# Eleven plain attention tiles instead of thirteen, and a new order of all operations

## The chip, the cores and the metric

The kernel runs on one core of a Trainium2 chip. The metric is the device time of one execution in microseconds. Three executions of the kernel before took 955.89, 956.62 and 960.74 us; the median is 956.62 us.

## What is computed

Inputs are q, k and v of 8 batches, 8 heads, 576 positions and 64 features in float32, and two weight matrices of 512x2048 and 2048x512 in float64. The reference, cut to what matters:

```python
scores = q @ k.T / 8                       # per batch and head
scores = where(0 <= row - col < 64, scores, -1e9)
attn = exp(scores - max); attn = attn / (sum(attn) + 1e-9)
x = (attn @ v), heads side by side         # 8 x 576 x 512
u = x + real(fft(fft(x, axis=1), axis=2))
un = (u - mean(u)) / sqrt(var(u) + 1e-6)   # over the 512 features
out = u + relu(un @ w_ch1) @ w_ch2
```

## The kernel before

The 4608 rows (8 batches of 576) are cut into 36 tiles of 128 rows; nine tiles make a pair of batches. Four kinds of work follow each other for each batch, and all of them share the engines:

- **attn_tile(T)**, 36 times: loads k, q and v of one tile, computes scores against the tile's own keys and the 64 before, the softmax, and the product with v. It also sums the four quarters of the features (`radix4`), and turns the result so that features lie along partitions (`flip_y` or `y_turn`).
- **fft(b)**, 8 times: both Fourier transforms of one batch as matrix products, written to a DRAM tensor `md`.
- **norm_tile(T)**, 36 times: gathers the rows of `md`, adds them to x, normalises, splits the result into two 16-bit parts and turns it by a DMA transpose (`u_turn`, L1271) into `uhl`, the input of the feed-forward part.
- **ffn(c)** and, for the last chunks, **ffn7(c)**: 18 chunks of two tiles each. In chunks 1 to 10 the first product is `bank1` (L1459, 16 groups of 12 matmuls) and the second is `second` (L1439, 16 groups of 6 for each half). Chunk 0 uses float32 weights. `weight_piece` makes float32 of the float64 weights on VectorE, and `weight_split` (L1414) makes two 16-bit parts.

An attention tile has two forms, chosen by `whole = T < PRO` in `attn_tile`:

- A **plain** tile (T below PRO) works in float32. TensorE transposes k and q against an identity (L491, four matmuls each), writes the mask into the score banks (L620, two) and adds the scores (L625, 32 float32 matmuls). VectorE takes the minimum (L644), ScalarE the exponentials (L657). TensorE transposes the probabilities (L674, eight), multiplies by v (L727, 32 float32 matmuls) and transposes the result (L840, four).
- A **split** tile writes every operand as a high and a low 16-bit part: the high part is a cast (L426 or L430, on ScalarE or VectorE), the low part a subtraction (L506, L517, L688 on GpSimd or VectorE; L561 on VectorE for v). The transposes of k, q, both halves of the probabilities and the result are five DMA transposes issued by SyncE. TensorE does the scores (L611, 32 float16 matmuls) and the product with v (L727, 48 float16 matmuls). VectorE does mask and minimum in one pass (L646, eight). Two copies per tile (`q_swap`) put q's low part beside its high part.

At T == PRO a few one-off operations turn the last plain tile's keys and values into two parts (`k_tail`, L546 to L549, and `v_tail`, L581 and L582), and `to_parts` negates the mask (L410).

The order of the instructions is made when the program is built. Each operation is given to `Plan.op` with an engine (or two to choose between, with a margin), a duration in us, the buffers it reads and writes, and a priority on a scale of us: `PITCH * T` for a tile, offsets for its steps, 60 and on for the weight splits, 1e6 and more for the feed-forward products, so that these come last. `Plan.order` is a list scheduler: it takes the operation that can start first by its model, and among these the one with the lowest priority. What it gives is a fixed order for every engine; on the chip each engine runs its list in that order and waits where an operand is late. In this schedule the feed-forward products fill TensorE wherever nothing of the other kinds is ready; where the model sees a gap before them, filler matmuls (`warm`, L1949) are put in.

Three tables change priorities without touching the work: `NUDGE` adds to the priority of the k-th operation of a kind, `LEAD` adds to all operations of a kind for one tile, piece or chunk, and `BIAS` adds to the margin by which the second engine is chosen. The key lookup that the change relies on is

```python
lead = LEAD.get({"split": "whole", "odd": "even", "first": "even"}.get(self.kind, self.kind), ())
prio += NUDGE.get(self.kind, {}).get(self.k, 0.0) + (lead[self.at] if self.at < len(lead) else 0.0)
```

and the choice between two engines is

```python
sooner = max(free[e2], s2) + d2 + o.margin < max(free[e1], s1) + d1
```

Of the kernel before, what the change touches and what calls it, by code (L numbers as in the profile page):

```python
# [41 lines left out]
LAZY_E, LAZY_Y = 0.3, 0.8  # L42
WARM = 0.8, 0.4
EARLY, LATER = 80, -20
PRO = 13
PITCH, FFT_AT, NORM_AT, FFT1 = 8.5, 13, 6, 0
SLACK = 0.0
SLACK_V = 0.3
WARY = 0
LAZY_N = 0.2  # L50
LAZY_S = 0.2
LAZY_Q = 0.1
LAZY_X = 1.0
# [12 lines left out]
ACT_NORM = 4  # L66
C_AT = ("fh", "fh", "pt", "pt")
NUDGE = {
    "": {0: 3.6, 1: 16.6, 2: -0.4, 3: 15.9, 4: 69.4, 5: 25.3, 6: -12, 8: 0.2, 10: 3.8, 11: -27.5},
}  # L70
LEAD = {
}
BIAS = {
}
VS = 64.0
YS = 32.0
# [78 lines left out]
class Plan:  # L155
# [21 lines left out]
    def op(self, eng, dur, prio, fn, reads=(), writes=(), lat=0.0, alt=(), holds=(), port=True, lock=True):  # L177

        o = Op()
        lead = LEAD.get({"split": "whole", "odd": "even", "first": "even"}.get(self.kind, self.kind), ())
        prio += NUDGE.get(self.kind, {}).get(self.k, 0.0) + (lead[self.at] if self.at < len(lead) else 0.0)
        o.group = (self.kind, self.at, self.k)
        bias = BIAS.get(self.kind, {}).get(self.k, 0.0)
        self.k += 1
        o.durs = {e: d + self.FIXED[e] for e, d in ([(eng, dur), alt[:2]] if alt else [(eng, dur)])}
        o.port, o.slack, o.wary, o.lock = port, self.slack, self.wary, lock
        o.margin = (alt[2] if len(alt) > 2 else self.MARGIN) + bias
        o.eng, o.dur, o.lat, o.fn, o.prio, o.margin = eng, dur, lat, fn, round(prio, 3), round(o.margin, 3)  # L190
        o.idx, o.outs, o.allocs = len(self.ops), [], []
        deps = set()
        for b in reads:
            deps.update(b.writers)
        for b in writes:
            deps.update(b.writers)
            deps.update(b.readers)
            if b.ring and not b.writers and b not in o.allocs:
                o.allocs.append(b)
        for b in holds:  # L200
            if b.ring and not b.held:
                o.allocs.append(b)
            b.held = True
        o.bufs = list({id(b): b for b in (*reads, *writes, *holds)}.values())
        for b in o.bufs:
            b.left += 1
        for b in reads:
            b.readers.append(o)
        for b in writes:

            b.writers.append(o)
        deps.discard(o)
        o.deps = deps
        self.ops.append(o)
        return o
# [116 lines left out]
def attn_fft_ffn_kernel(ctx: ExitStack, tc: tile.TileContext, q, k, v, w1, w2, gidx, dft_d, dft_s, mask, out):  # L332
# [72 lines left out]
    def to_parts():  # L405
# [5 lines left out]

        op("POOL", 0.4, PITCH * PRO - 25, negate, writes=[Bmskb], lock=False)

# [21 lines left out]
    def attn_tile(T, base):  # L435
        pb, n = divmod(T, NT)
        b0, i = 2 * pb, T % 2
        own, old = T % 3, (T + 1 if T == PRO else T - 1) % 3

        whole = T < PRO  # L440
        lazy = plan.MARGIN if whole else LAZY
# [27 lines left out]

        before = (T + 1 if T == PRO else T - 1) % 3  # L470
        kst_ = (kst32 if whole else kst16)[:, T % 3 * kw : (T % 3 + 1) * kw].rearrange("p (h s) -> p h s", s=P)
# [63 lines left out]
        was = plan.k  # L535
        if T == PRO and n > 0:

# [35 lines left out]
        was = plan.k  # L573
        if T == PRO:
            last = (T - 1) % 3
# [162 lines left out]

        op("DVE", 0.62, base + 6.25, normed, [bpa, brc], [bx], alt=("ACT", 2.6, LAZY_N), port=False)
        plan.k += 1  # L740
# [1240 lines left out]
```

## Time and profile before

| | us |
|---|---|
| executions, three | 955.89, 956.62, 960.74 |
| the profiled execution's own time | 960.97 |
| its span, first to last instruction | 959.2 |
| TensorE busy | 940.1 (98%) |
| VectorE busy | 806.8 (84%) |
| ScalarE busy | 588.5 (61%) |
| GpSimd busy | 297.0 (31%) |
| mean granted TensorE clock | 0.996 |

PE is TensorE, PEld its weight loads, DVE VectorE, ACT ScalarE, POOL GpSimd, SP SyncE, which issues nearly all DMAs. "L727" is line 727 of the kernel, and tile names stand as out<-in. Busy times of matmuls are modelled with their pipeline's tail, so two groups in a row overlap a little; in the chain of waits the steps are counted from start to start and do not overlap.

### The profile page before, as it was taken

To read this page: it belongs to the slowest core of one execution; us is meant where nothing else is said; L and a number is where in the kernel's file an instruction comes from. 1 tells how busy PE (TensorE), PEld (TensorE's weight loads), DVE (VectorE), ACT (ScalarE), POOL (GpSimd) and SP (SyncE) were. 2 spreads that over 40 slices of the span, in tenths; PEclk is the share of its full clock that TensorE was granted. 3 is DMA by queue.
4 is the path that set the end of the run, shared out by engine and by line. 5 is a ranking of instruction groups with operands and counts; after the bars stand their busy time and mean duration, and the time that the engine had idled before them with its cause. 6 is when DMAs were issued, how large, how long until landed. Compare 5 with 4: busy or idle time off the path is not lost.

```text
span 959.2 us, 25735 instructions
## 1 busy us (share of the span) xinstructions
PE 940.1 (98%) x10209; PEld 729.7 (76%) x10209; DVE 806.8 (84%) x1894; ACT 588.5 (61%) x1540; POOL 297.0 (31%) x335
## 2 busy tenths in 40 slices
PE   8999999999999999999899999999999999999997
PEld 6777767767776767677676676676688999999996
DVE  4989898998977988977986997989977688888685
ACT  6866768887767586866576773343454555645352
POOL 1111020343534342523422352332110254534040
PEclk9999999999999999999999999999999999999999
DMA  8979941599899699989969563312123213222000
GB/s 192 298 175 272 284 110 45 140 168 204 166 217 201 148 204 190 213 179 204 166 164 204 116 150 91 100 28 75 25 65 80 60 62 74 59 81 43 21 23 24
DMA packets 302697, 127.60 MB, mean 133 GB/s; under 512 B 281064, under 2 KB 281704, under 8 KB 302576
## 3 DMA queue, kind: packets, MB, share of 16 engines
q1 hardware_dynamic: 299712, 116.91, 55.0%
q0 software_dynamic: 2720, 8.92, 3.5%
q8 instruction: 80, 1.31, 0.6%
q14 instruction: 41, 0.34, 0.1%
q10 hardware_dynamic: 144, 0.13, 0.0%
HBM read 62.85 MB, written 22.04 MB: 89 GB/s over the span
## 4 chain that ended last, share of the span: by engine, by line
PE 76%; DVE 10%; DMA 6%; ACT 3%; issue 3%; POOL 2%; POOLq 0%; SPq 0%; DVEq 0%; ACTq 0%
PE ph L1459 19%; PE po L1439 18%; PE q L1815 11%; PE py L1707 5%; PE ph L1680 4%; PE px L1707 4%; PE pa L727 2%; PE pz L1047 2%; PE psc L611 2%; PE pg L995 2%; DMA out<-xu 2%; PE pp L674 1%; DMA xu<-xd 1%; PE psc L625 1%; ACT pr L657 1%
## 5 line engine op out<-in xcount | busy, mean ns | idle before, releaser
L1439 PE MATMUL po<-w1s,hh 128*128 128x512 f16 (+1 forms) x1024 | 264.5, 393 | 0.0
L1459 PE MATMUL ph<-uhl,w0s 128*128 128x256 f16 (+1 forms) x2040 | 263.2, 279 | 0.0
L1459 PEld LDWEIGHTS <-w0s 128*128 128x128 f16 x1920 | 186.5, 98 | 50.5 <-issue 1.1
L1439 PEld LDWEIGHTS <-hh 128*128 128x128 f16 x960 | 91.4, 98 | 81.3 <-issue 1.2
L1198 POOL DMA_INDIRECT mt<-md,gix x34 | 41.9, 1233 | 127.9 <-DVE xu L1211 58.4
L1471 ACT ACTIVATE hh<-ph 128x512 f16<-128x512 f32 x80 | 47.2, 590 | 49.7 <-PE po L1439 24.7
L1474 DVE SCALAR_TENSOR_TENSOR hh<-ph,hh 128x512 f16<-128x512 f32 x80 | 54.6, 683 | 21.1 <-ACT hh L1471 20.8
L657 ACT ACTIVATE pr<-pr,nm 128x128 f32<-128x128 f32 x184 | 71.3, 391 | 1.4 <-DVE nm L646 1.2
L1815 PEld LDWEIGHTS <-qbd 128*128 128x128 f16 x672 | 64.7, 98 | 9.1 <-DVE qbd L1779 1.1
L1815 PEld LDWEIGHTS <-kst 128*128 128x128 f16 x504 | 49.2, 98 | 5.7
L1779 DVE TENSOR_TENSOR flex<-flex 128x256 f32<-128x256 f32 x92 | 39.9, 434 | 9.5 <-ACT flex L1750 3.7
L430 POOL COPY yp<-y 128x1024 uint16<-128x1024 uint16 x23 | 25.5, 1109 | 70.7 <-DVE y L762 58.1
L1707 PEld LDWEIGHTS <-wa 128*128 128x128 f16 x750 | 45.9, 98 | 0.2
L1707 PEld LDWEIGHTS <-w0s 128*128 128x128 f16 x720 | 44.9, 98 | 0.2
L646 DVE CUSTOM_DVE_ANT_0 pr<-psc,mskb 128x128 f32<-128x128 f32 x184 | 42.0, 283 | 2.3 <-PE psc L611 2.2
L1680 PE MATMUL ph<-uhl,w0s 128*128 128x256 f16 x384 | 43.7, 273 | 0.0
L1224 POOL TENSOR_TENSOR rs<-mv,mhalf 128x1 f32<-128x1 f32 x36 | 26.1, 726 | 55.1 <-DVE mv L1220 52.5
L1815 PE MATMUL q<-w1s,qbd 128*128 128x256 f16 x336 | 41.4, 273 | 1.4 <-DVE qbd L1779 0.9
L1680 PEld LDWEIGHTS <-w0s 128*128 128x128 f16 x384 | 37.6, 98 | 5.4
L1792 ACT CAST qbd<-flex 128x1024 f16<-128x1024 f32 x28 | 29.2, 1044 | 19.6 <-DVE flex L1779 11.6
L1707 PE MATMUL py<-uhl,wa 128*128 128x128 f16 x570 | 41.0, 219 | 0.0
L426 ACT COPY v<-v 64x1024 uint16<-64x1024 uint16 x25 | 26.1, 1044 | 23.8 <-PE pa L727 20.9
(278 smaller groups left out, 2147.9 us busy)
## 6 DMA issues: line engine op xcount, KB each, us to landing
wd<-in_moe_w_ch SPq DMA_DIRECT2D x26, 512.0 KB
out<-xu SPq DMA_DIRECT2D x34, 256.0 KB
kn<-in_k SPq DMA_DIRECT2D x32, 256.0 KB
qn<-in_q SPq DMA_DIRECT2D x32, 256.0 KB
xd<-xa SPq DMA_DIRECT2D x30, 256.0 KB
xu<-xd SPq DMA_DIRECT2D x30, 256.0 KB
flex<-in_v SPq DMA_DIRECT2D x20, 256.0 KB
md<-mp SPq DMA_DIRECT2D x24, 192.0 KB
```

The lines of the kernel that those rows point to most:

```text
L646: nc.vector.tensor_tensor_reduce(out=t["pr", jj][:, hp], in0=t["ps", jj][:, hp], in1=mskb[:, m : m + P], scale=-0.125, scalar=3.0e38, op0= ...
L657: nc.scalar.activation(pr, src, AF.Exp, bias=t["nm", jj][:, hp : hp + 1], scale=-1.0, accum_out=t["rc"][:, hp, jj])
L1198: nc.gpsimd.indirect_dma_start(out=mts[T], out_offset=None, in_=mds[pb][0 : HR if n < 4 else 2 * HR], in_offset=bass.IndirectOffsetOnAxis( ...
L1439: nc.tensor.matmul(t["po"][i], l_, r_, start=(f == 0 and x == 0), stop=(f == NKF - 1 and x == len(mm) - 1))
L1459: nc.tensor.matmul(ph, l_, r_, start=(x == 0), stop=(x == len(mm) - 1))
L1471: nc.scalar.activation(t["hh", pr][:, 0], ph, AF.Relu)
L1474: nc.vector.scalar_tensor_tensor(out=hh[:, 1], in0=ph, scalar=0.0, in1=hh[:, 0], op0=ALU.max, op1=ALU.subtract)
L1680: nc.tensor.matmul(ph, l_, r_, start=(x == 0), stop=(x == len(mm) - 1))
L1707: nc.tensor.matmul(to[:, x], l_(a, k_), r_(b_, k_), start=(y == 0), stop=(y == 5))
L1779: return lambda eng=nc.vector: eng.tensor_tensor(out=o, in0=a, in1=b, op=al)
L1792: op("ACT", 0.95, -9, lambda h4=h4, oa=oa: nc.scalar.copy(oa[:, 0], h4), Bh4, [Boa])
L1815: nc.tensor.matmul(t["q"][q_][:, y], l_[:, a, i, m], r_(b_, m), start=(s_ + y + m + x == 0), stop=(s_ == 3 and m == 1 and x == 2 and (y == ...
```

## The change

`PRO` goes from 13 to 11: tiles 11 and 12 are made as split tiles. `LAZY_N`, the margin by which the scaling of the attention output (`normed`) goes to ScalarE rather than VectorE, goes from 0.2 to -0.8. The three tables get entries for nearly all kinds of operations.

```diff
-PRO = 13
+PRO = 11
...
-LAZY_N = 0.2
+LAZY_N = -0.8
...
 NUDGE = {
-    "": {0: 3.6, 1: 16.6, 2: -0.4, 3: 15.9, 4: 69.4, 5: 25.3, 6: -12, 8: 0.2, 10: 3.8, 11: -27.5},
+    "": {0: 14.4, 1: 16.6, 2: -0.4, 3: 15.9, 4: 69.4, 5: 25.3, 6: -12, 8: 0.2, 10: 3.8, 11: -27.5},
+    "even": {14: -0.3},
+    "ffn7": {16: -0.6, 232: 0.3, 1276: 3.2, 2005: 0.6, 2006: 0.7, 2047: 12.4, 2100: -0.7, 2120: 1.3, 2141: -0.3, 2145: -0.1, 2146: 0.5, 2167: 0.2},
+    "first": {21: 0.8, 32: -0.1, 62: 1.2},
+    "odd": {34: -2.9},
+    "piece": {0: 10.6},
+    "split": {3: -0.1, 25: -0.2},
 }
 LEAD = {
...
+    "norm": (
+        0, 0, 0, 0, 0, 0, 0, 0, 0, 0.4, 0, 0, 0, 0, 2.6, 2.6,
+        3.9, 3.9, 3.9, 4, 3.9, 4.1, 3.9, 3.9, 3.9, 3.9, 3.9, 3.9, 3.9, 3.9, 3.9, 3.9,
+        3.9, 3.9, 3.9, 3.9,
+    ),
+    "part": (
+        0.3, 0.3, 0.3, 0.3, 0.3, 0.3, 0.3, 0.3, 0.3, 0.3, 0.3, 0.3, 0.3, 0.3, 0.3, 0.3,
+        0.3, 0.3, 0.3, 0.3, -1.7, 0.3, 0.3, 0.3, 0.3, 0.3, 0.3, 0.3, 0.3, 0.3, 0.3, 0.3,
+    ),
+    "piece": (
+        0, 0, 0, 0, 0, 0, 0, 0, 0, 0, 0, 0, 0, 0, 0, 0,
+        0, 0, 0, 0, 0, 0, 0, 0, 0, 0.1, 0, 0.8, 0.8, 0.8, -9.9, -9.9,
+    ),
...
+    "whole": (
+        0, 0, 0, 0, -1.5, -1.5, -1.5, -1.5, -2.9, -2.9, -2.9, -2.9, -2.9, -2.9, -2.9, -2.9,
+        -2.9, -2.9, -2.9, -2.9, -4.6, -2.9, -2.9, -2.9, -2.9, -2.9, -2.9, -2.9, -2.9, -2.9, -2.9, -2.9,
+        -2.9, -2.9, -3.1, -3.1,
+    ),
 }
 BIAS = {
+    "ffn7": {21: -0.4},
+    "first": {13: -0.8},
 }
```

The tables left out here hold zeros only.

## Rows read from the trace of the kernel before

**Rows 1.** Busy time of engines by stage: window, length, each engine, PEclk, DMA share, GB/s.
```profile
0.00:87.00 87.00, 81.71 (x956) 62.52 (x957) 68.51 (x144) 61.00 (x215) 16.01 (x25) 1.00 0.86 229
87.00:130.00 43.00, 43.00 (x295) 30.76 (x295) 39.00 (x80) 28.05 (x92) 4.48 (x4) 1.00 0.81 236
130.00:190.00 60.00, 59.45 (x499) 42.93 (x499) 55.21 (x111) 47.79 (x115) 12.45 (x11) 1.00 0.39 99
190.00:214.00 24.00, 23.70 (x233) 16.12 (x231) 21.98 (x70) 20.80 (x62) 10.73 (x15) 1.00 0.88 177
214.00:460.00 246.00, 244.87 (x2849) 174.81 (x2847) 207.26 (x588) 173.58 (x467) 99.19 (x110) 1.00 0.98 191
460.00:520.00 60.00, 54.76 (x610) 39.76 (x609) 51.04 (x151) 41.09 (x113) 18.76 (x20) 0.94 0.84 178
520.00:955.00 435.00, 432.57 (x4779) 362.84 (x4776) 362.97 (x754) 216.18 (x480) 134.83 (x150) 1.00 0.28 67
```
**Rows 2.** What TensorE waited for: total us, times, longest.
```profile
PE pg L995 <- DVE hs L955: 3.9, 4, 2.9
PE pa L727 <- DMA pt<-flex: 2.0, 1, 2.0
```
**Rows 3.** Chain of waits, plain tiles on TensorE, 123 to 178: start, us, what.
```profile
123.94 0.87 PE pp L674 x8
...
131.88 0.44 PE pk L491 x4
...
139.86 0.43 PE psc L620 x2
140.29 1.03 PE psc L625 x32
...
176.33 1.08 PE pa L727 x32
```
**Rows 4.** The same chain, split tiles and chunk 1's last products, 204 to 220.
```profile
204.90 0.57 PE psc L611 x16
...
215.37 1.29 PE po L1439 x6
...
217.97 0.88 PE pa L727 x48
218.85 0.90 PE psc L611 x32
```
**Rows 5.** Instructions by line: count, busy us, mean ns, idle before them.
```profile
L646 DVE CUSTOM_DVE_ANT_0 pr<-psc,mskb 128x128 f32<-128x128 f32 x184 | 42.0, 283 | 2.3 <-PE psc L611 2.2
...
L644 DVE TENSOR_REDUCE nm<-psc 128x4 f32<-128x512 f32 x26 | 16.8, 683 | 12.2 <-PE psc L625 12.2
...
L561 DVE SCALAR_TENSOR_TENSOR v<-flex,v 128x512 f16<-128x512 f32 x23 | 18.8, 819 | 2.2 <-ACT v L559 2.2
...
L688 DVE TENSOR_TENSOR flex<-pr,flex 128x512 f16<-128x512 f32 x26 | 20.6, 801 | 1.6 <-ACT flex L426 1.3
...
L688 POOL TENSOR_TENSOR flex<-pr,flex 128x512 f16<-128x512 f32 x20 | 25.7, 1286 | 25.7 <-ACT flex L426 17.7 <-DVE flex L430 6.3 <-DVE sw L1532 1.6
```
**Rows 6.** Timeline, VectorE and GpSimd, 165 to 168: start, us, what.
```profile
165.01 0.75 DVE L1414 SCALAR_TENSOR_TENSOR w1s<-w1s,s 128x512 f16<-128x512 f32 x1
...
166.85 1.70 DVE L1414 SCALAR_TENSOR_TENSOR w0s<-w0s,s 128x512 f16<-128x512 f32 x1
166.84 1.15 POOL L517 TENSOR_TENSOR flex<-qn,flex 128x512 f16<-128x512 f32 x1 [27.39 <-DVE flex L430]
```
**Rows 7.** Timeline around chunk 2's start: SyncE's issue of its last transpose, TensorE's first use.
```profile
207.72 1.24 SPq L1271 DMA_TRANSPOSE uhl<-up  x1
...
213.90 1.47 PE L1459 MATMUL ph<-uhl,w0s 128*128 128x256 f16 x12
```
**Rows 8.** Chain of waits, DMA transposes at 290 and 505, issue to landing.
```profile
290.75 4.95 DMA uhl<-up
...
505.58 6.03 DMA pt<-flex
```

More of the change, by code (lines that the diff above doesn't have):

```diff
@@ L68 @@
 NUDGE = {
-    "": {0: 3.6, 1: 16.6, 2: -0.4, 3: 15.9, 4: 69.4, 5: 25.3, 6: -12, 8: 0.2, 10: 3.8, 11: -27.5},
+    "": {0: 14.4, 1: 16.6, 2: -0.4, 3: 15.9, 4: 69.4, 5: 25.3, 6: -12, 8: 0.2, 10: 3.8, 11: -27.5},
[5 more added lines that the diff above has]
+    "split": {3: -0.1, 25: -0.2},
 }
 LEAD = {
+    "": (
+        0,
+    ),
+    "even": (
+        0, 0, 0, 0, 0, 0, 0, 0,
+    ),
+    "ffn7": (
+        0, 0, 0, 0, 0, 0, 0, 0, 0, 0, 0, 0, 0, 0, 0, 0,
+        0, 0,
+    ),
[7 more added lines that the diff above has]
+        0.3, 0.3, 0.3, 0.3, -1.7, 0.3, 0.3, 0.3, 0.3, 0.3, 0.3, 0.3, 0.3, 0.3, 0.3, 0.3,
+    ),
+    "piece": (
+        0, 0, 0, 0, 0, 0, 0, 0, 0, 0, 0, 0, 0, 0, 0, 0,
+        0, 0, 0, 0, 0, 0, 0, 0, 0, 0.1, 0, 0.8, 0.8, 0.8, -9.9, -9.9,
+    ),
+    "pre1": (
+        0, 0, 0, 0,
+    ),
+    "prep": (
+        0, 0, 0, 0,
+    ),
+    "scale": (
+        0, 0,
+    ),
+    "tail": (
+        0, 0, 0, 0, 0, 0, 0, 0, 0, 0, 0, 0,
+    ),
+    "whole": (
+        0, 0, 0, 0, -1.5, -1.5, -1.5, -1.5, -2.9, -2.9, -2.9, -2.9, -2.9, -2.9, -2.9, -2.9,
+        -2.9, -2.9, -2.9, -2.9, -4.6, -2.9, -2.9, -2.9, -2.9, -2.9, -2.9, -2.9, -2.9, -2.9, -2.9, -2.9,
+        -2.9, -2.9, -3.1, -3.1,
+    ),
 }
 BIAS = {
+    "ffn7": {21: -0.4},
+    "first": {13: -0.8},
 }
```

## The prediction

> **What bounds the kernel now.** I read the busy times by stage first, then what TensorE waited for, then the chain of waits. In the stages the reader is to see that TensorE is the full engine from 87 us on: 43.00 of 43, 59.45 of 60, 23.70 of 24, 244.87 of 246, and 432.57 of 435 from 520 to 955 [rows 1]. One stage is different: from 460 to 520 it is busy for 54.76 of 60 at a granted clock of 0.94. The waits name the two stalls in it: 3.9 us for an FFT operand (2.9 of them at once), 2.0 us for a transposed probability tile [rows 2]. Before 87 us, 81.71 of 87 are busy, but this includes filler matmuls; there the chain through attention tiles, the first FFT and the weights sets the pace. So, from 87 us on, a matmul that is taken out shortens the run by its length, provided that the list behind it can move up. The second engine to watch is VectorE: 39.00 of 43, 55.21 of 60 and 21.98 of 24, which leaves 4.00 + 4.79 + 2.02 = 10.8 us of idle time between 87 and 214 [rows 1]. The two tiles that change form lie there.
>
> **Part 1: TensorE loses work.** A plain tile costs, from start to start in the chain: k turned 0.44, q and the result, four matmuls of the same shape each, 0.44 each; mask 0.43; scores 1.03; probabilities turned 0.87; product with v 1.08 [rows 3]. The sum is 4.73 us. A split tile costs 0.90 for its scores in one piece, or 2 x 0.57 in two, and 0.88 for the product with v [rows 4]: 1.78 to 2.02, middle 1.90. One tile saves 2.71 to 2.95, two save 5.4 to 5.9; I take 2 x 2.83 = 5.7 us. All of these matmuls lie after 105 and before 214, where TensorE is full, so they are on the path.
>
> **Part 2: VectorE, ScalarE, GpSimd and DMA gain work.** On VectorE, mask and minimum take 8 x 42.0/184 = 1.83 us per tile instead of 2 x 16.8/26 = 1.29, so 0.54 more; the low part of v adds 18.8/23 = 0.82; the low parts of k, q and the two halves of the probabilities are four subtractions of one shape, 20.6/26 = 0.79 each on VectorE or 25.7/20 = 1.29 each on GpSimd [rows 5]. On GpSimd they are not free for VectorE: the subtraction at 166.84 held GpSimd for 1.15 us, and the weight split that VectorE started beside it took 1.70 instead of 0.75 [rows 6]. So a tile adds between 0.54 + 0.82 + 4 x 0.79 = 4.5 and 0.54 + 0.82 + 4 x 1.29 = 6.5 us of VectorE's time, two tiles 9.0 to 13.0. Some copies out of PSUM that VectorE did for plain tiles fall away, and the new `LAZY_N` sends scalings to ScalarE, which has 12.21 us idle in 130 to 190 against VectorE's 4.79 [rows 1]. I take the lower end, 9.0, which the 10.8 us of idle time hold; then this costs nothing. If it does not fit, the price is in the third rival.
>
> The Trainium skill has a rule that speaks against this part, in "SBUF — State Buffer", section "Who interferes with whom": VectorE and GpSimd share one pair of ports, held for a whole instruction, and the loser waits instead of sharing. The 1.70 us agree. By the rule all eight low parts would cost VectorE 1.29 each wherever they run, and part 2 would come to 13.0.
>
> The DMA side gets ten more transposes, and no load falls away. One takes 1.24 us of SyncE's time to issue [rows 7] and 4.95 us from issue to landing in a crowded stretch [rows 8], so ten take between 12 and 50 us of the queue. From 130 to 190 the DMA engines are busy 0.39 of the time, which leaves 37 us [rows 1]. I take 30, about the middle, which that gap hides. Without the cover (from 190 on the share is 0.88, then 0.98) a transpose lands as late as the one at 505, 6.03 us after issue, and that one was the stall of 2.0 us [rows 8, 2].
>
> **Part 3: what is late next.** TensorE would reach the products of chunk 2 5.7 us earlier, at 213.90 - 5.7 = 208.2, but their last operand leaves SyncE only at 207.72 [rows 7] and lands, at 4.95 us [rows 8], at 212.7. Uncovered, that is a wait of 4.5 us, and the change would keep 1.2 us. The cover is what stands behind chunk 2's start and needs nothing of it: two groups of chunk 1's second product, 1.29 each, and the attention products of 0.88 and 0.90 [rows 4], together 4.4 us, which can go first. Moving the FFT of batch 1 and the gathers of tiles 4 and 5 up would serve as well. I cost this at nothing, between 0 and 4.5.
>
> **Part 4: the new order.** The tables add no instruction. They redraw the whole list, so the small stalls fall elsewhere. What they can win after 87 us is what TensorE does not use now: 5.24 us idle from 460 to 520, with up to 0.06 x 60 = 3.6 us lost to the clock, together 8.8; 2.43 after 520; 1.98 between 87 and 460 [rows 1]. What they can lose I bound by as much again, 8.8. The `norm` entries of 3.9 make the gathers of tiles 16 and on later against the rest, and those of `whole` make attention earlier; both move work inside a stretch that TensorE fills with feed-forward products anyway. In the first 87 us at most the 5.29 idle us and some fillers could go. I take nothing for part 4, the middle between its ends, since the rows show no stall that the model must have seen.
>
> **The sum.** The profiled execution took 960.97 us, of which 959.2 are the span. 960.97 - 5.7 = 955.3. The median of the three executions is 4.35 us lower than this one, 956.62, and the saved matmuls are the same in any of them: 956.6 - 5.7 = 950.9 us.
>
> **The rivals.**
>
> The first: the order also removes the stalls of 460 to 520. For it speaks that both hang on one late operand each; against it that the list is fixed from a model which did not see them. Time: 950.9 - 8.8 = 942.1.
>
> The second: the gate in part 3 is not covered. TensorE arrives early at chunk 2 and waits for the transposed rows of tile 5. For it speaks that the operand's landing at 212.7 is only 1.2 us ahead of its use now, and that VectorE, which makes it, is at 92% from 130 to 190. Against it, the 4.4 us of products that can go first. Time: 956.6 - 1.2 = 955.4.
>
> The third, on the other side: VectorE cannot hold the extra work between 87 and 214. At 13.0 us against 10.8 of idle time it no longer fits, and one tile's 6.5 us standing ahead of the FFT of batch 1 puts the landing off to 212.7 + 6.5 = 219.2. TensorE, with the 4.4 us of part 3, is done at 208.2 + 4.4 = 212.6 and waits 6.6 us. The clock's loss comes on top: in 460 to 520 it was up to 3.6 for 5.24 idle us [rows 1], so here up to 4.5. Against the saving of 5.7 this is +5.4 us: 962.0. It decides where VectorE's added work passes its idle time by more than the 2 to 3 us that the copies and scalings give back. For it speaks [rows 6]; against it that tile 12 has a lower claim in the list than the FFT of batch 1.
>
> That the edit would leave the two tiles plain is excluded by `whole = T < PRO`.
>
> **How the numbers follow.** 0.5% is 4.8 us, about what a measurement of this kernel can tell from no change: faster is below 951.8, slower above 961.4. The forecast has 0.54, with its own range 946 to 955 (parts 1 and 3 by their ends, part 4 by half of its); 0.35 of it is faster, 0.19 is the same. The first rival has 0.16, all faster. The second has 0.16, 0.02 of it faster and 0.14 the same. The third has 0.14, 0.13 of it slower and 0.01 the same. Together faster 0.53, same 0.34, slower 0.13. The range from 942 to 959 leaves out half of the first rival and most of the third.
>
> **What would show it.** Part 1: 64 matmuls of L625 less and 64 of L611 more, and nothing of L491, L620 or L625 after 130. Part 2: VectorE busy in 87 to 214 by about 9 us more, with TensorE's share there not below 0.98; DMA busy share from 130 to 190 well above 0.39. Part 3: chunk 2's first product at 208 to 210 with no wait before it; a wait of over 2 us there with the last `uhl` transpose before it speaks for the second rival, one for an FFT operand or a weight split before 214 for the third. Part 4: the waits of TensorE after 214 as long in total as before. The prediction is wrong if TensorE's first products of the feed-forward part start at another time than 87, since then the early stage, on which I counted nothing, has moved.

## The result and the profile after

The changed kernel took 946.15 us (median of 4, 943.76 to 946.86) against 956.78 (median of 4, 955.89 to 960.74) for the kernel before in the same series. By the medians it is faster by 10.6 us. The measured ratio, 0.9866 with a 95% interval of 0.9839 to 0.9893, is not that of the two medians (0.9889): it puts the gain at 12.8 us, 10.2 to 15.4. A second series, below, gives 0.9888, which is 10.7 us. The forecast was 5.7: the direction is right and the time lies between 942 and 959, but the gain is about twice the one named. One execution of 1757 us, of the kernel with the matmuls put back below, is left out of its times.

The page after, as [rows 1] and the text around them read the page of before: engines with busy us, share of the span and instructions, then the hardware queue's share of the DMA engines. The profiled execution took 946.62 us, its span 944.8.

```profile
PE 928.9 (98%) x10193; PEld 720.3 (76%) x10193; DVE 800.1 (85%) x1922; ACT 594.5 (63%) x1545; POOL 313.6 (33%) x348
...
q1 hardware_dynamic: 310272, 119.53, 59.1%
```

Before, these stood at 940.1, 806.8 (DVE), 588.5 (ACT), 297.0 (POOL) and 55.0%. TensorE lost 11.2 us of busy time; VectorE lost 6.7 although the form adds work to it; GpSimd has 16.6 and ScalarE 6.0 more.

The stages after, columns as in [rows 1]; the last window ends where TensorE's work now ends.

```profile
0.00:87.00 87.00, 80.46 (x939) 61.72 (x943) 67.69 (x144) 60.63 (x214) 13.91 (x25) 1.00 0.88 231
87.00:130.00 43.00, 43.00 (x282) 30.04 (x275) 39.01 (x80) 25.43 (x80) 7.53 (x7) 1.00 0.79 220
130.00:190.00 60.00, 60.00 (x486) 42.62 (x484) 51.13 (x107) 46.90 (x100) 11.63 (x12) 1.00 0.40 100
190.00:214.00 24.00, 23.63 (x236) 16.32 (x233) 20.84 (x67) 21.91 (x62) 10.02 (x14) 1.00 0.82 160
214.00:460.00 246.00, 243.21 (x2855) 172.73 (x2854) 210.96 (x620) 178.35 (x484) 106.25 (x116) 1.00 1.04 201
460.00:520.00 60.00, 59.89 (x713) 42.45 (x713) 51.03 (x141) 42.81 (x116) 22.82 (x22) 1.00 1.02 194
520.00:941.00 421.00, 418.72 (x4708) 354.39 (x4702) 358.93 (x766) 218.47 (x495) 141.28 (x154) 1.00 0.30 69
```

Two things stand out against [rows 1]. The stage from 460 to 520 is full now, 59.89 of 60 at a clock of 1.00, where it was 54.76 at 0.94. And VectorE between 87 and 214 is busy for 39.01 + 51.13 + 20.84 = 111.0 us, 5.2 less than the 116.2 before, while its share from 214 to 460 rose by 3.7.

What TensorE waited for, against [rows 2]: total us, times, longest.

```profile
PE warm L1997 <- POOL ident masks.py:199: 2.1, 1, 2.1
PE ph L1507 <- DVE hh L1522: 1.3, 1, 1.3
PE ph L1507 <- DMA uhl<-up: 1.1, 2, 0.7
PE pp L722 <- ACT pr L705: 1.1, 3, 0.5
PE pa L775 <- DMA pt<-flex: 0.9, 2, 0.6
```

The 3.9 us for the FFT operand are gone, the 2.0 for the probability tile are 0.9. The longest wait after 87 us is 1.3, for a hidden tile (`hh`) of the feed-forward part.

Groups of instructions of the attention tiles, as in [rows 5] (a line of after is 48 above its line of before):

```profile
L694 DVE CUSTOM_DVE_ANT_0 pr<-psc,mskb 128x128 f32<-128x128 f32 x200 | 45.5, 282 | 0.6 <-PE psc L659 0.5
...
L736 POOL TENSOR_TENSOR flex<-pr,flex 128x512 f16<-128x512 f32 x20 | 26.8, 1342 | 24.4 <-ACT flex L474 19.0 <-DVE flex L478 5.0 <-DMA pt<-flex 0.4
L736 DVE TENSOR_TENSOR flex<-pr,flex 128x512 f16<-128x512 f32 x30 | 21.4, 715 | 0.7 <-ACT flex L474 0.4
L609 DVE SCALAR_TENSOR_TENSOR v<-flex,v 128x512 f16<-128x512 f32 x25 | 17.5, 701 | 0.0
...
L692 DVE TENSOR_REDUCE nm<-psc 128x4 f32<-128x512 f32 x22 | 14.2, 684 | 12.0 <-PE psc L673 11.9
L673 PE MATMUL psc<-kst,qbd 64*64 64x128 f32 x352 | 12.1, 275 | 0.0
```

The form did what it says: 64 single-precision score matmuls fewer (352 after 416), 16 mask instructions more (200 after 184), two low parts of v more (25 after 23). The low parts of k and q on VectorE, before and after, and the scalings on ScalarE, one instruction a head, so one tile:

```profile
L506 DVE TENSOR_TENSOR flex<-kn,flex 128x512 f16<-128x512 f32 x13 | 10.3, 796 | 1.1 <-ACT flex L426 1.0
L517 DVE TENSOR_TENSOR flex<-qn,flex 128x512 f16<-128x512 f32 x8 | 6.5, 807 | 0.6 <-ACT flex L426 0.4
...
L554 DVE TENSOR_TENSOR flex<-kn,flex 128x512 f16<-128x512 f32 x15 | 11.2, 749 | 0.4 <-ACT flex L474 0.2
L565 DVE TENSOR_TENSOR flex<-qn,flex 128x512 f16<-128x512 f32 x11 | 8.6, 783 | 0.2
...
L735 ACT ACTIVATE xa<-pa,rc 128x64 f32<-128x64 f32 x8 | 1.7, 309 | 0.0
...
L783 ACT ACTIVATE xa<-pa,rc 128x64 f32<-128x64 f32 x8 | 1.7, 329 | 0.2 <-PE pa L775 0.2
```

With those of the probabilities (26 and 30) VectorE runs 56 such subtractions instead of 47, GpSimd 44 instead of 45: all of the new ones went to VectorE. And the new margin sends no more scalings to ScalarE than the old one, one tile of 36.

Chunk 2's gate, the counterpart of [rows 7]: start, us, what.

```profile
198.63 1.23 SPq L1319 DMA_TRANSPOSE uhl<-up  x1
...
202.94 1.25 PE L1507 MATMUL ph<-uhl,w0s 128*128 128x256 f16 x10 [0.37 <-DMA uhl<-up]
```

The last transpose leaves SyncE 9.1 us earlier than before, the first product starts 11.0 us earlier and waits 0.37 for it. The feed-forward part itself starts at 83.2 instead of 86.8.

### The profile page after: what moved, and what is told of

It is laid out like the page before. It is cut to its first block, busy times and chain, and to the rows that moved or that the text cites. A ratio compares the mean times of both kernels' runs of the same rounds, so it can differ in the third digit from the quotient of the medians.

```text
span 944.8 us, 25747 instructions
## 1 busy us (share of the span) xinstructions
PE 928.9 (98%) x10193; PEld 720.3 (76%) x10193; DVE 800.1 (85%) x1922; ACT 594.5 (63%) x1545; POOL 313.6 (33%) x348
## 4 chain that ended last, share of the span: by engine, by line
PE 75%; DVE 10%; DMA 6%; issue 5%; ACT 3%; POOL 1%; SPq 1%; POOLq 0%; ACTq 0%; DVEq 0%
PE ph L1507 19%; PE po L1487 19%; PE q L1863 11%; PE py L1755 5%; PE ph L1728 4%; PE px L1755 4%; PE pa L775 3%; PE pg L1043 2%; DMA pt<-flex 2%; PE psc L659 2%; PE pz L1095 2%; DMA mt<-md,gix 1%; DVE y L810 1%; PE pp L722 1%; ACT pr L705 1%
## 5 line engine op out<-in xcount | busy, mean ns | idle before, releaser
L705 ACT ACTIVATE pr<-pr,nm 128x128 f32<-128x128 f32 x200 | 77.5, 391 | 1.9 <-DVE nm L694 1.8
L478 POOL COPY yp<-y 128x1024 uint16<-128x1024 uint16 x24 | 28.7, 1195 | 73.4 <-DVE y L810 52.2
L694 DVE CUSTOM_DVE_ANT_0 pr<-psc,mskb 128x128 f32<-128x128 f32 x200 | 45.5, 282 | 0.6 <-PE psc L659 0.5
L1798 ACT ACTIVATE flex<-flex 128x384 f32<-128x384 f32 x40 | 20.7, 518 | 37.2 <-DVE flex L1778 37.1
L474 ACT COPY qbd<-qbd 64x1024 uint16<-64x1024 uint16 x40 | 41.7, 1043 | 2.7 <-DMA qbd<-flex 1.7
L478 POOL COPY yT<-py 128x1024 uint16<-128x1024 uint16 (+2 forms) x24 | 26.5, 1107 | 47.7 <-DMA py<-yp 45.0
```

Source lines behind the costliest of these rows:

```text
L474: nc.scalar.mul(out, in_, scale) if scale is not None else nc.scalar.copy(out, in_)
L478: eng.tensor_copy(out, in_)
L694: nc.vector.tensor_tensor_reduce(out=t["pr", jj][:, hp], in0=t["ps", jj][:, hp], in1=mskb[:, m : m + P], scale=-0.125, scalar=3.0e38, op0= ...
L705: nc.scalar.activation(pr, src, AF.Exp, bias=t["nm", jj][:, hp : hp + 1], scale=-1.0, accum_out=t["rc"][:, hp, jj])
```

## The experiments

Each kernel was timed beside the kernel before on the same chip; a ratio is to that one, with its 95% interval.

**What repeats.** The kernel before again, unchanged, for a second profile:

> The kernel before, unchanged, profiled a second time. Theory A (my account: 5.7 us are the two tiles' TensorE work, the rest is stalls of the fixed list, 2.9 us at 476 and 2.0 at 511 with 3.4 us of half clock behind them): both stalls come back at the same places, and the span is again near 959. Rival B (the stalls belong to one execution only, not to the list): the stalls are absent or elsewhere, and the span is near 955.

It took 958.75 us, ratio 1.0012 [0.9999, 1.0025]. The profile, of 956.09 us, shows waits and the stage of [rows 2] and [rows 1]:

```profile
PE pz L1047 <- DVE g L1005: 2.5, 4, 1.5
PE pg L995 <- DVE hs L955: 1.6, 3, 0.9
...
PE pa L727 <- DMA pt<-flex: 0.6, 1, 0.6
...
460.00:520.00 60.00, 56.70 (x633) 41.06 (x631) 48.98 (x151) 42.09 (x120) 18.78 (x20) 0.97 0.77 172
```

Waits at the same operands are back in the same stage, in other sizes: the one for the FFT operand `hs` is 0.9 instead of 2.9, with 1.5 for the next one, `g`, behind it; the one for the probability tile is 0.6 instead of 2.0; 3.30 us are idle instead of 5.24. The span, 954.3, is nearer to what Rival B named than to Theory A's 959. So the places belong to the list, and the lengths to the execution.

The changed kernel again:

> The changed kernel, unchanged, as the base for the next two on the same chip. All theories: 944 to 948 us, and no stall over 1.5 us after 87 us.

945.61 us, 0.9888 [0.9865, 0.9911]; no wait over 1 us after 87 and 59.90 of 60 busy from 460 to 520.

**The matmuls put back.** The changed kernel with 52 matmuls that nothing reads ahead of the scores of tiles 11 and 12, in the same order:

```diff
             new_scores(x)
+            for _ in range(13 if T < 13 else 0):
+                nc.tensor.matmul(t["ps", x][:, 0:2], ident[:].bitcast(F16)[:, 0:P], ident[:].bitcast(F16), start=True, stop=True)
```

> The changed kernel, its order untouched, with 13 more matmuls of 256 columns (L1949's shape, about 0.11 us each) ahead of each of the four score blocks of tiles 11 and 12: 52 x 0.109 = 5.7 us of TensorE put back where the plain form was taken out. The scores overwrite what they write. Theory A (TensorE is the bound there, work counts one for one): 5 to 6 us above the changed kernel, 951 to 952. Rival C (TensorE waits there for VectorE anyway, and the form gave nothing): 0 to 2 us above, 946 to 948.

950.18 us, 0.9925 [0.991, 0.9941], so 4.6 us above the changed kernel by the medians and 3.5 by the two ratios. In its timeline the added group of 13 stands at 189.02 and the scores follow:

```profile
189.02 1.58 PE L656 MATMUL psc<-ident 128*128 128x256 f16 x13
190.53 0.64 PE L661 MATMUL psc<-kst,qbd 128*64 128x128 f16 x16
```

The 52 took 6.06 us from start to start. A microsecond of work on TensorE here is 0.6 to 0.8 of one at the end: less than Theory A's 5 to 6 us, more than Rival C's 0 to 2. The intervals of the ratios, about 0.2% each way, leave room for the full 6.06.

**The form and the tables, each alone.** The changed kernel with 13 plain tiles:

```diff
-PRO = 11
+PRO = 13
```

> The changed kernel with thirteen plain tiles again: the new tables and margin alone. Theory A: 946 + 5.7 = 951 to 953, if the list so made has no large stall. Rival C (the tables bring all): 946 to 948. Rival D (the tables bring nothing, the form all 10.6 us): 955 to 958.

963.33 us, 1.0053 [1.0033, 1.0073]. The new tables and margin without the form make the kernel slower, which none of the three theories had (they end at 958). Five waits for probability tiles and three for hidden tiles are new:

```profile
PE pa L775 <- DMA pt<-flex: 3.5, 5, 1.2
PE po L1487 <- DVE hh L1522: 3.3, 3, 1.7
...
460.00:520.00 60.00, 55.17 (x645) 39.62 (x643) 51.56 (x151) 44.71 (x115) 23.90 (x25) 1.00 0.92 183
```

The run gives something else: the work of the form by itself, since it differs from the changed kernel in nothing else and neither lost clock while TensorE had work. Summed from start to start by line, the lines of plain tiles cost TensorE 9.69 us less in the changed kernel (mask, single-precision scores, the product with v, and the turning of k, q, the probabilities and the result), those of split tiles 3.71 more: 5.98 for two tiles.

The form without the tables, in the kernel before:

```diff
-PRO = 13
+PRO = 11
```

> The kernel before with PRO = 11 and nothing else: the old tables and margin. Theory A (the form is worth 5 to 6 us, the rest of the 10.6 is how large the stalls of one particular list are): 951 to 953 if its list stalls as much as that of before, anything from 946 to 960 otherwise, and time less TensorE's idle and half-clock loss equal to that of the changed kernel within 2 us. Rival D (the form brings all): 945 to 948.

978.83 us, 1.0224 [1.02, 1.0249]: 20.8 us slower, with 6 us less to do, and far outside Theory A's 946 to 960. TensorE is busy for 18.02 of 24 us from 190 to 214. The chain there says why:

```profile
200.44 5.95 DMA uhl<-up
...
206.51 1.15 POOL yp L430
...
207.67 1.25 SPq L851
...
208.98 4.38 DMA pt<-flex
213.35 6.29 DMA uhl<-up
```

SyncE issues its transposes in the order of the list. The one for the probability tile, whose operand VectorE had finished by 202.8 at the latest, stands behind one that waits for GpSimd's copy, and that copy starts when the transpose before it has landed. It leaves at 208.98 and lands at 213.35, and chunk 2's operand lands 6.3 us behind it. TensorE waited 5.89 and 4.11 us for probability tiles, and its granted clock was half for 10.24 us from 212 on. The rest of the loss lies in the last layer's projections: waits of 6.63 us at 764 and 2.89 at 811, with another 17 us at half clock between 761 and 816. The second half of Theory A held: this time less TensorE's idle time and less half of its busy time at half clock is 936.3, against 935.7 and 935.5 in the two profiles of the changed kernel. The form's work was saved, and the waits cost more.

The form with the new margin for the scalings:

```diff
-PRO = 13
+PRO = 11
...
-LAZY_N = 0.2
+LAZY_N = -0.8
```

> The kernel before with PRO = 11 and LAZY_N = -0.8, the three tables as before. Theory A: as for the form alone, 946 to 960 with its own stalls. Rival E (the margin, which takes scalings off VectorE, is what removes the stalls): 946 to 948, and fewer stalls on VectorE than with the form alone.

953.82 us, 0.9964 [0.9943, 0.9985]. The waits of the last layer are gone, the gate is there (start, us, what, idle time before and its releaser):

```profile
203.12 2.76 PE L1439 MATMUL po<-w1s,hh 128*128 128x512 f16 x12
207.88 0.28 PE L727 MATMUL pa<-v,pt 128*64 128x64 f16 x6 [2.00 <-DMA pt<-flex]
...
210.79 1.33 PE L727 MATMUL pa<-v,pt 128*64 128x64 f16 x42 [2.62 <-DMA pt<-flex]
...
213.13 3.17 PE L1459 MATMUL ph<-uhl,w0s 128*128 128x256 f16 x14 [1.01 <-DMA uhl<-up]
```

Chunk 2 starts at 213.1, as before the change (213.90): TensorE is idle for 5.6 us in front of it, 4.6 of them for a probability tile and 1.0 for chunk 2's rows. A stretch of 6.8 us at half clock came on top; TensorE was busy for 4.5 of it and so lost 2.3.

The margin alone:

```diff
-LAZY_N = 0.2
+LAZY_N = -0.8
```

> The kernel before with LAZY_N = -0.8 alone. Theory A: within 6 us of before to either side, since the list is another one. Rival E: 4 to 5 us below before, with less busy time of VectorE and no FFT stall after 460.

957.94 us, 1.0012 [0.999, 1.0035]: no gain. The stall from 460 to 520 is gone (60.00 busy), one of 5.0 us stands at 791 instead.

**The port at the FFT stall.** The kernel before in its order, with the low parts of k and q of one tile moved from GpSimd to VectorE:

```diff
+    low = [0]
+
+    def place_low(eng):
+        if eng is nc.gpsimd:
+            low[0] += 1
+            return nc.vector if low[0] in (36, 37) else eng
+        return eng
...
+                eng = place_low(eng)
```

> The kernel before, its order untouched, with two subtractions (the low parts of one tile's k and q that GpSimd ran at 468.7 to 471.6 us, just when VectorE's three L955 took 4.26 us) done on VectorE at the same place of the list. Theory F (the FFT stall of 2.9 us at 476 is VectorE held up by GpSimd on the port that both share): VectorE has the two subtractions of 0.6 each instead of 2.8 us of being held, the stall shrinks to 1.5 us or less, time 1 to 3 us below before. Rival G (VectorE is late there for its own amount of work): the stall grows by 1.2 us, time the same or 1 to 2 us above.

957.71 us, 0.9993 [0.9978, 1.0008]. The first three rows are of the kernel before, VectorE and GpSimd side by side:

```profile
467.76 4.26 DVE L955 SCALAR_TENSOR_TENSOR fs<-f,fs 128x388 f16<-128x388 f32 x3
...
468.70 1.46 POOL L506 TENSOR_TENSOR flex<-kn,flex 128x512 f16<-128x512 f32 x1
470.13 1.47 POOL L517 TENSOR_TENSOR flex<-qn,flex 128x512 f16<-128x512 f32 x1
```

And of this kernel:

```profile
464.42 2.34 DVE L966 SCALAR_TENSOR_TENSOR fs<-f,fs 128x388 f16<-128x388 f32 x3
...
468.47 0.68 DVE L515 TENSOR_TENSOR flex<-kn,flex 128x512 f16<-128x512 f32 x1
```

With both subtractions on VectorE the three take 2.34 us instead of 4.26, and the wait for the FFT operand `hs` is 0.7 in total. Theory F held for the three instructions. For the time it is not shown: the ratio allows a gain of 0.2% at most, and the second profile of the kernel before has the same 4.26 with a longest wait of 0.9 there. Whether the hold is a part of the stall stays open; it does not set its length alone. The Trainium skill ("SBUF — State Buffer", "Who interferes with whom") says that VectorE contends with a reading GpSimd instruction where it takes two inputs from SBUF; these do, and the 1.9 us agree.

**Which table.** The changed kernel with the old `NUDGE` and an empty `BIAS`, so with `LEAD` alone:

```diff
 NUDGE = {
-    "": {0: 14.4, 1: 16.6, 2: -0.4, 3: 15.9, 4: 69.4, 5: 25.3, 6: -12, 8: 0.2, 10: 3.8, 11: -27.5},
...
+    "": {0: 3.6, 1: 16.6, 2: -0.4, 3: 15.9, 4: 69.4, 5: 25.3, 6: -12, 8: 0.2, 10: 3.8, 11: -27.5},
 }
...
-    "ffn7": {21: -0.4},
-    "first": {13: -0.8},
```

> The changed kernel with the old NUDGE and an empty BIAS: of the tables LEAD alone (whole, norm, part, piece), beside PRO = 11 and the margin. Theory A2 (after the form and margin runs: the 5.7 us are kept only if the list brings chunk 2's rows and the split tiles' transposes before TensorE gets there, near 205 us; with the old tables it waited there 10 and 7 us with 5.1 and 3.4 us of half clock): whichever table does that gives 944 to 948 and shows no wait over 1.5 us between 200 and 220. If LEAD does it: so here. If not: a wait there, and 951 to 956. Rival E2 (the waits are spread over the list, no one place): somewhere between, with small waits all along.

946.04 us, 0.9889 [0.9855, 0.9923]: the changed kernel's gain in the series above. With `NUDGE` and `BIAS` new and `LEAD` empty:

```diff
-    "norm": (
...
-    "part": (
...
-    "piece": (
...
-    "whole": (
...
```

> The changed kernel with an empty LEAD: of the tables NUDGE and BIAS alone, beside PRO = 11 and the margin. Theory A2: the other half of the run before; if the early part of LEAD (attention from tile 4 on 1.5 to 2.9 us sooner) is what clears the gate near 205 us, a wait of 5 us or more stands there and the time is 951 to 956. Rival E2: between 946 and 953, small waits all along.

953.72 us, 0.997 [0.9937, 1.0003], with executions from 950.4 to 962.3; the profile is of one of 959.81. The gate is back, at 190 to 214 TensorE is busy for 18.45 of 24:

```profile
PE pa L735 <- DMA pt<-flex: 6.7, 7, 2.0
PE ph L1467 <- DMA uhl<-up: 3.9, 1, 3.9
```

**Other numbers of plain tiles, same tables.** With 12:

```diff
-PRO = 11
+PRO = 12
```

> The changed kernel with twelve plain tiles: new tables, one tile in the other form. Theory A2 (work counts 2.8 to 3 us a tile, the rest is the list's own waits): 946 + 3 = 949 if its list waits as little as that of the changed kernel; each us of wait and half clock in its trace on top. Rival D2 (the tables need eleven): 955 or more.

955.0 us, 0.9964 [0.9939, 0.999], 2.1 us of waits each for an FFT operand and a probability tile. That is Rival D2's bound, but Theory A2 reaches it too: 949, and 3.7 to 6.4 us more idle time on TensorE than in the changed kernel's profiles. With 10:

```diff
-PRO = 11
+PRO = 10
```

> The changed kernel with ten plain tiles: one tile more in split form. By TensorE's work alone 946 - 3 = 943. Theory A2: VectorE, SyncE and GpSimd have one more split tile before chunk 2's rows, the gate near 205 us opens later, and TensorE waits there again: 948 to 958, with the wait between 195 and 220. Rival H (any tile fewer gains): 942 to 944.

972.65 us, 1.0157 [1.0121, 1.0193]. Theory A2 had the place, but its range ended at 958. One wait of 11.8 us:

```profile
217.19 0.38 PE L775 MATMUL pa<-v,pt 128*64 128x64 f16 x6 [11.79 <-DMA pt<-flex]
...
222.98 2.72 PE L1507 MATMUL ph<-uhl,w0s 128*128 128x256 f16 x12 [3.43 <-DMA uhl<-up]
```

By the sum of part 1 a third tile in the new form would save about 3 us of TensorE's work; the list made for 11 tiles pays 15.2 us of waits at the gate for it, and 17 us at half clock from 209 on.

**Whether the gate swallows the work.** If the wait at chunk 2 had eaten the saving, the same 52 matmuls put into the kernel with form and margin should cost nothing there:

```diff
-PRO = 13
+PRO = 11
...
-LAZY_N = 0.2
+LAZY_N = -0.8
...
+            for _ in range(13 if T < 13 else 0):
+                nc.tensor.matmul(t["ps", x][:, 0:2], ident[:].bitcast(F16)[:, 0:P], ident[:].bitcast(F16), start=True, stop=True)
```

> The kernel of the form and the margin, old tables, its order untouched, with the same 52 matmuls (5.7 us) ahead of the scores of tiles 11 and 12 as in the put-back run on the changed kernel. These scores run at 153 and 176 us, ahead of the place near 207 where that list waits 6.7 us with 3.4 us of half clock behind. Theory K (the wait near 207 is TensorE arriving early: it swallows what the form gave): the wait shrinks by 4 to 6 us and the time is 0 to 2 us above the 953.8 of the run without the matmuls. Rival L (the wait is independent of when TensorE arrives): 5 to 6 us above, 959 to 960, with the same wait.

959.96 us, 1.002 [0.9998, 1.0043]: 6.1 us more than without them, or 5.4 by the two ratios, since this was another chip. That is their full length of 6.06, or nearly. Theory K fell:

```profile
222.68 2.53 PE L1461 MATMUL ph<-uhl,w0s 128*128 128x256 f16 x11 [4.18 <-DMA uhl<-up]
```

The gate moved along, from 213.13 to 222.68, and still waits: chunk 2's operand leaves SyncE at 218.15 instead of 209.32. The likely reason, argued and not tried, is that the late operands descend from the scores that the matmuls delay. So the 6 us of the form were in the time of that list too, under its own waits: 10.3 us of idle time after 87, where the two profiles of before have 9.1 and 7.3.

**Which entries of the table.** Three kernels from the one with form and margin, with `LEAD` entries added: `whole`; `whole`, `piece` and `part`; `piece` and `part`.

```diff
+    "whole": (
+        0, 0, 0, 0, -1.5, -1.5, -1.5, -1.5, -2.9, -2.9, -2.9, -2.9, -2.9, -2.9, -2.9, -2.9,
...
```

> Of LEAD the entries of the attention tiles alone (whole), beside PRO = 11 and the margin. Theory M (one entry, that of attention tiles, clears the gate near 205 us): 944 to 948. Rival N (a list is good or bad as a whole, parts of the table are no parts of the gain): not below 952, with waits of several us somewhere.

965.8 us, 1.0074 [1.0045, 1.0102]: no wait over 0.8 us is left near 207, but 11.5 us are waited at 757 to 770. The gate is cleared, as Theory M had it, and the time is Rival N's.

```diff
+    "whole": (
...
+    "piece": (
...
+    "part": (
...
```

> Of LEAD the attention tiles' entries and those of the weights (whole, piece, part); norm left out. Theory M: 944 to 948, as with the attention tiles' entries alone. Rival N: 944 to 948 only if norm changes nothing in the list; else 950 or more.

945.27 us, 0.9888 [0.9849, 0.9926]: the changed kernel's time, without `norm`.

```diff
+    "piece": (
...
+    "part": (
...
```

> Of LEAD the entries of the weights alone (piece and part). Theory M: as the form and margin alone, 951 to 956. Rival N: anywhere from 946 to 975, with waits at other places than near 207.

971.26 us, 1.0162 [1.0118, 1.0206], with the longest wait of these three:

```profile
PE px L1715 <- DMA uhl<-up: 12.8, 2, 9.6
```

By the ratios, against 0.9964 without entries, the two parts cost 1.1% and 2.0%, each by itself, and win 0.8% together. The entries have no prices of their own that could be added; only a whole list has one.

## Where the prediction was right, and why it failed

**Part 1 held.** 5.7 us were worked out for two tiles; the lines of two kernels with the same tables give 5.98, and putting 6.06 us of work back costs 3.5 to 4.6 in the one list and 5.4 to 6.1 in the other. The principle behind it, that from 87 us on a matmul taken out shortens the run by its length provided that the list can move up, held with that proviso: 0.6 to 1.

**Part 2 had the wrong place, and its end was right.** VectorE was to gain 9 us between 87 and 214 and lost 5.2. The list moved the two tiles back: their scores stood at 140 and 178, and now the first ones stand at 189 and 197. VectorE took all new low parts, but later. In return eight sums of `radix4`, 4.8 us, and other work stand on GpSimd; the scalings that I counted on for ScalarE did not move. The DMA share from 130 to 190 was to go well above 0.39 and is 0.40; the gap that I named as the transposes' cover isn't used: four are issued there as before, and nine of the ten more between 214 and 460, where the share is 1.04 instead of 0.98. No operand came late for it by more than 1 us, so costing it at nothing was right, for a reason that I didn't give. The third rival, VectorE overrun, did not come about in the changed kernel.

**Part 3 had the place, its mechanism fell.** With form and margin and the old tables the products of chunk 2 start at 213.1, against a forecast landing of 212.7; the waits before it are 5.6 us against the second rival's 4.5, and the time is 953.82 against its 955.4. That these numbers are near is luck. I had TensorE arrive early at an operand that lands at a fixed time; but only 1.0 of the 5.6 us is a wait for that operand, and with the 52 matmuls put back the landing moved along. Of the cover that I named, the two groups of chunk 1's second product did go first (the 2.76 us at 203.12), and the attention product was itself the late one. In the changed kernel the chain that feeds the gate runs 9.1 us earlier, so chunk 2 starts at 202.94 and not at 208 to 210.

**Part 4 failed.** "I take nothing for part 4, the middle between its ends, since the rows show no stall that the model must have seen." The term measured about 4.7 us by the medians, 10.6 less 6.0 for the form, and 6.8 by the measured ratio. It closes on the traces. The first profile of before has 13.05 us of idle time on TensorE and 3.4 lost to two stretches at half clock, at 478 and 512, the second one 10.4 and 1.7. Profiles of the changed kernel have 9.2 and 6.5, and no half clock while TensorE had work. So the list gives back 3.9 us of idle time and 1.7 to 3.4 of clock. With the form's 5.98 this is 11.6 of the 12.3 us between the shorter spans (954.3, 942.0), and 13.3 of the 14.4 between the longer ones (959.2, 944.8). The rest, about 1 us, is in the busy time of other lines (fillers are 49 after 53), which fell by 1.4 to 1.7, less a first matmul that comes 0.7 later.

The sign that I had set for this part came: after 214 TensorE was idle for 8.3 and 6.4 us in the profiles of before, and is for 4.3 and 1.9. So did the one for the early stage: the feed-forward part starts at 83.2. But the gain is not made there: of the first 87 us TensorE is idle for 6.5 and 6.7, where it was for 5.3 and 4.5.

That is the first rival's mechanism, the stalls of 460 to 520 removed, at half to three quarters of the price that I gave it (8.8), and I gave it 0.16. The error was in the reasoning, not in a row: the idle time and the half clock of [rows 1] are a cost of one list, and a change that redraws the list throws that cost away and draws a new one. Nothing was the middle of the bounds, but the new draw was not an even one. The bounds themselves were too narrow: lists for 11 plain tiles ran from 945.3 to 978.8 us here, while I allowed a loss of 8.8. Most of what sets these times apart is waits and clock: TensorE's busy time, less half of what it did at half clock, is 936.6 and 936.1 us in the profiles of before, 928.9 and 928.7 in those of the changed kernel, and 928.2 to 933.5 in the other lists for 11 plain tiles with the new margin or without.

**What stays open.** Why the margin and the two groups of `LEAD` entries work only together; in what the executions of one list differ so that its stall is 2.9 us in one and 0.9 in another; whether a list made for 10 plain tiles would gain again; and how the gain divides between the form and the tables, since the tables without the form lose. The removal of waits can't be split into stalls either: none was taken out alone with a measurable gain.

## What to carry to other kernels

Work taken from an engine that is full counted here at 0.6 to 1 of its length, but where each engine runs a list in order, the change must be judged with a list made for it: form alone +20.8 us, tables and margin alone +5.3, all together -10.6. Read the idle time and the half clock of the full engine as what the present list loses and a new one may give back or double, and give that term a price and a spread of its own. Then look for the operands that arrive just in time at the next stage, and at the in-order queue that issues them: there one late transpose cost more than the form won.

## What the hardware showed beside

- A wait of TensorE can cost more than itself: waits of 2.00 and 2.62 us close together came with 6.8 us at 1.2 GHz, waits of 11.79 and 3.43 with 17 us at it. One of 1.72, in the kernel with twelve plain tiles, came with none.
- The same instructions in the same order stalled for 2.9 us in one execution and for 0.9, with 1.5 at the next operand, in another, at the same hold of 4.26 us on VectorE.
- A DMA transpose queued on SyncE behind one that waits for GpSimd left at least 6.2 us after its own operand was written; it landed at 213.35, and the operand behind it 6.29 us later still.
